# Two buffers for the mix's tile, 25-row stores as 24 and 1, and weights converted in 8 chunks

## The chip, the cores and the metric

The kernel runs on one core of one Trainium2 chip. The metric is the device time of one execution in microseconds (us). Five engines work side by side, each in the order of its own instruction list: TensorE (PE, with its weight loads as PEld), VectorE (DVE), ScalarE (ACT), GpSimd (POOL) and SyncE (SP), which here issues every DMA. An instruction that waits holds up all that stand behind it on its engine.

## The reference, cut to what matters

```python
X = rfft(x, axis=1)                        # x: 8 x 3136 x 256
Yr = shrink(Xr @ w_r - Xi @ w_i + b_r)     # shrink: towards zero by 0.01
Yi = shrink(Xr @ w_i + Xi @ w_r + b_i)
y  = irfft(Yr + 1j*Yi, n=3136, axis=1)
mixed = real(fft(fft(y, axis=1), axis=2))
u  = y + mixed
un = (u - mean(u)) / sqrt(var(u) + 1e-6)   # over the 256 features
out = u + relu(un @ w_ch1) @ w_ch2         # 256 -> 1024 -> 256, weights float64
```

The sequence transform of y is Y itself, so `mixed` needs only a transform of Y over the 256 features. The two MLP weights come as float64 and are turned on the chip into a high and a low float32r part.

## The kernel before, in words

The length 3136 is factored as 64 x 49. Each of 8 batches (b) goes through ten generators, one per stage:

- `p1`: the 64-point transform. A chunk of `x` is loaded into `xf`, multiplied (`g_f`), copied to `ev` and stored to a DRAM array `ad` (L348 to L367). For batch 0 it is `p1_first` (L279 to L334), whose copies use borrowed tiles, the tags `uth`, `utl` and `W0` among them. From each copy the first eight frequencies are stored at once and the rest later (the `rest` stores, L333).
- `p2_f2`: the 49-point transform, in four quarters q of eight frequencies. `af` and `tff` are loaded (L400, L402), the product `g_f` (L416) is split into `Xh`, `Xl`, `Xsh`, `Xsl`. The tiles come from `x_tiles`: in quarters 1 and 3 of batch 0 they are borrowed, the two `Xh` from tag `uth` (written by L429), the two `Xl` from `utl`.
- `p2_w`: the complex weights, bias and shrink, giving `Y` (L470 to L481).
- `p2_mix`: the feature transform of Y, for `mixed`. Even and odd parts (`ef` or `eo`, L516), four products `g_mix` (L535 to L540), each copied into a quarter of the tile `mq` (by ACT at L542 in batch 0, by DVE at L546 after), sums and differences (L548 to L557), and stores of `mq` into the DRAM array `md` (L562 to L574).
- `p2_yt`, `p2_g2`: transposes of Y and the inverse 49-point transform, `bev`, stored to `bd` (L637).
- `p3_norm`: loads `bf` from `bd` (L664) and `mt` from `md` (L668, L670), the inverse 64-point transform `g_g`, the sum `ut` (L678), the normalization (L683 to L695).
- `p3_tr`, `p3_mlp1`, `p3_mlp2`: transposes into `uth`, `utl` (tags of the same names, two buffers each, L705), the two MLP products (`h` and `o`), the sum and the output store (L752, L754).

`weights` (L756) drives `split_double` (L158) for the float64 weights: 16 chunks of 256 columns each. A chunk is loaded as pairs of 32-bit words into `raw` (tag `bf`, two buffers, L166), eight DVE instructions work on the words (L169 to L182), ACT makes the high part (L183), POOL the low part (L185, L186). `behind(1, ...)` puts the load on SP behind the load of batch 0's second `af` tile.

Order. Every generator yields due times in units of T (a batch takes 1.0 T in steady state, and the weights lie at 1.2 T to 1.7 T); a heap emits the instructions in the order of the due times (L774 to L780). The tile framework then plans each engine's list from that sequence with a simulated timeline, takes a buffer of a tag when one is free, and puts in the semaphores. So the order of each engine's list is a result of planned times, and tags with a fixed number of buffers are what a tile waits for. Stores and loads share SP's one queue.

The lines of `x_tiles` that borrow:

```python
if b == 0 and q % 2:
    return [[sb.tile([128, 8] + c + [S], F32R, tag=t + z, bufs=2, ...) for k in range(2)]
            for t, c in (("ut", [2]), ("b", [])) for z in "hl"]
```

Of the kernel before, what the change touches and what calls it, by code (L numbers as in the profile page):

```python
# [10 lines left out]
F32 = mybir.dt.float32  # L11
F32R = mybir.dt.float32r
I32 = mybir.dt.int32
AF = mybir.ActivationFunctionType
ALU = mybir.AluOpType
# [104 lines left out]
T = 10000  # L120
# [8 lines left out]
def spectral_block(ctx: ExitStack, tc: tile.TileContext, x, w_ri, b_ri, w1, w2,  # L129
# [3 lines left out]
    va, sc, gp, te = nc.vector, nc.scalar, nc.gpsimd, nc.tensor  # L133
# [21 lines left out]
    st_eng = nc.sync  # L155


    def split_double(name, h, l, sl, src):  # L158

        def tmp(tag, bufs, dt=I32):
            return sb.tile([128, 256], dt, tag=tag, bufs=bufs, name=f"cv_{name}_{tag}")

        raw = sb.tile([128, 512], I32, tag="bf", bufs=2, name="raw_" + name)
        behind(1, out=raw, in_=src)  # L166
        lo, hi = raw[:, 0::2], raw[:, 1::2]
        t = tmp("mt", 2)
        va.tensor_scalar(t, hi, 0x7FFFFFFF, None, op0=ALU.bitwise_and)  # L169
        tf = t.bitcast(F32)  # L170
        va.tensor_scalar(tf, tf, HI_MIN, HI_MAX, op0=ALU.max, op1=ALU.min)
        va.tensor_scalar(t, t, 3, 0x7FFFFFFF, op0=ALU.logical_shift_left, op1=ALU.bitwise_and)
        w = tmp("ut", UTB)
        va.tensor_scalar(w, hi, -0x80000000, 0x40000000, op0=ALU.bitwise_and, op1=ALU.bitwise_or)
        va.tensor_tensor(w, w, t, op=ALU.bitwise_xor)
        wf = w.bitcast(F32)
        e = tmp("ut", UTB)
        va.tensor_scalar(e, w, -0x800000, None, op0=ALU.bitwise_and)
        r = tmp("mt", 2)
        va.tensor_scalar(r, lo, 8, None, op0=ALU.logical_shift_right)  # L180
        rf = tmp("ut", UTB, F32)
        va.scalar_tensor_tensor(rf, r, 2.0 ** -44, e.bitcast(F32), op0=ALU.mult, op1=ALU.mult)  # L182
        sc.copy(h[sl], wf)  # L183
        d = tmp("ut", UTB, F32)
        gp.tensor_sub(d, wf, h[sl].bitcast(F32))  # L185
        gp.tensor_add(l[sl], d, rf)  # L186


    fwd_f = cp.tile([128, 128], F32, name="fwd_f")
# [65 lines left out]
    def behind(key, **kw):  # L255

        assert key in af_ld
        with tc.issue_after(af_ld[key]):
            return nc.sync.dma_start(**kw)
# [227 lines left out]
    def p2_mix(b):  # L487


        md = dr.tile([2 * (NH + 64), D], F32, tag="md", bufs=4, name=f"md{b}")  # L490
        mpd, mmd = m_dram[b] = md[0:NH + 64], md[NH + 64:]
        both = md[0:2 * (NH + 63)].rearrange("(a r) d -> a r d", a=2)

        def rows(d, first, nj, n):

            return d[first:first + 64 * nj].rearrange("(j k) d -> j k d", k=64)[:, 0:n]

        def rows2(first, nj):
            return both[:, first:first + 64 * nj].rearrange("a (j k) d -> j a (k d)", k=64)[:, :, 0:4 * D]
        for q in range(4):  # L500
            base, STEP, F2W, W0, WW, M0 = clock2(b, q)
            u0 = 8 * q
            yield base + STEP * M0
            y = yt_[b, q]
            if b == 0:
                ef = sb.tile([128, 2, 8, S], F32, tag=("eh", "el")[q % 2], bufs=1, name="ef")
            else:
                eh = sb.tile([128, 2, 4, 100], F32R, tag="eh", bufs=1, name="eh")
                el = sb.tile([128, 2, 4, 100], F32R, tag="el", bufs=1, name="el")


            sets = ((np.s_[:], np.s_[:25]), (np.s_[::-1], np.s_[25:]))
            for e in range(2):
                eo = sb.tile([128, 8, S], F32, tag="eo", bufs=2, name="eo") if b else ef[:, e]
                for ru, js in sets:
                    va.scalar_tensor_tensor(eo[:, :, js], y[:, 1, ru, e, js], mask[:, e:e + 1],  # L516
                                            y[:, 0, ru, e, js], op0=ALU.mult, op1=ALU.add)
                    if e:
                        sc.copy(eo[0:1, :, js], y[0:1, 1, ru, 0, js])
                if b:  # L520
                    eov = eo.rearrange("p (u s) j -> p u (s j)", s=2)
                    sc.copy(eh[:, e], eov)
                    lo_v(el[:, e], eov, eh[:, e])

            mq = sb.tile([100, 2, 4, 2, 128], F32, tag="mq", bufs=1, name="mq")
            even, odd = mq[:, 1, :, 0], mq[:, 1, :, 1]
            for ui in range(4):
                yield base + STEP * (M0 + 0.372 + 0.394 * ui / 2)
                g = gtile("g_mix")
                gv = g[:100].rearrange("p (c h e) -> p c h e", c=2, h=2)  # L530
                for e in range(2):
                    o = g[:100, e * 256:e * 256 + 256]
                    n = (129, 128)[e]
                    if b == 0:
                        te.matmul(o[:, :n], ef[:, e, 2 * ui:2 * ui + 2].rearrange("p s j -> p (s j)"), KF["cs"][:, e, :n], start=True, stop=True)  # L535
                    else:
                        cs = K["cs"][:, e].rearrange("p h e -> p (h e)")
                        te.matmul(o, eh[:, e, ui], cs, start=e == 0, stop=False)
                        n += n % 2
                        te.matmul(o[:, :n], el[:, e, ui], cs[:, :n], start=False, stop=e == 1)  # L540
                if b == 0:
                    sc.copy(mq[:, 1, ui], gv[:, :, 0])  # L542
                else:
                    low = lows[ui % 2]
                    sc.copy(low[:, :, 1:], gv[:, :, 1, 1:])
                    va.tensor_add(mq[:, 1, ui], gv[:, :, 0], low)  # L546

                va.tensor_add(mq[:, 0, ui, 1, 0:1], gv[:, 0, 1, 0:1], odd[:, ui, 0:1])  # L548

            for i, f in ((0, va.tensor_add), (1, va.tensor_sub)):  # L550
                f(even[:, :, i::2], even[:, :, i::2], odd[:, :, 0:1].to_broadcast((100, 4, 64)))
            gp.tensor_add(mq[:, 0, :, 0, 1:], even[:, :, 1:], odd[:, :, 1:])
            gp.tensor_sub(mq[:, 0, :, 1, 1:], even[:, :, 1:], odd[:, :, 1:])
            sc.copy(mq[:, 0, :, 0, 0:1], even[:, :, 0:1])
            sc.copy(even[:, :, 1:], mq[:, 0, :, 1, 1:])
            va.tensor_copy(odd[:, :, 1:], mq[:, 0, :, 0, 1:])
            sc.copy(odd[:, :, 0:1], mq[:, 0, :, 1, 0:1])  # L557
            mr = mq.rearrange("p a u h e -> p a (u h e)")
            mp, mm = (mq[:, i].rearrange("p u h e -> p u (h e)") for i in range(2))

            if q:
                st_eng.dma_start(out=rows2(u0, 25), in_=mr[0:25])  # L562
                st_eng.dma_start(out=rows2(61 - u0, 24), in_=mr[75:99])
            else:
                st_eng.dma_start(out=rows(mpd, 0, 25, 4), in_=mp[0:25])
                st_eng.dma_start(out=rows(mmd, 0, 25, 3), in_=mm[0:25, 1:4])
                st_eng.dma_start(out=rows(mpd, 61, 24, 3), in_=mp[75:99, 0:3])
                st_eng.dma_start(out=rows(mmd, 60, 24, 3), in_=mm[75:99, 0:3])

                st_eng.dma_start(out=rows(mmd, 63, 24, 1), in_=mm[1:25, 0:1])  # L570
                st_eng.dma_start(out=rows(mpd, 32, 24, 1), in_=mp[75:99, 3:4])
                st_eng.dma_start(out=rows(mmd, 31, 25, 1), in_=mm[75:100, 3:4])
            st_eng.dma_start(out=rows2(u0 + 4, 25), in_=mr[50:75])
            st_eng.dma_start(out=rows2(57 - u0, 24), in_=mr[25:49])  # L574
        done.add(("m", b))

# [177 lines left out]
                st_eng.dma_start(out=out[b // 2, :, slot:slot + n, :], in_=ut[:, :n])  # L754

    def weights():  # L756
        w1v = w1.bitcast(I32).rearrange("(k p) f -> k p f", p=128)
        w2v = w2.bitcast(I32).rearrange("(f p) e -> f p e", p=128)
        parts1 = [(np.s_[:, k, q * 256:q * 256 + 256], w1v[k, :, q * 512:q * 512 + 512])
                  for k in range(2) for q in range(4)]  # L760
        parts2 = [(np.s_[:, f, :], w2v[f]) for f in range(8)]
        for i, (name, shape, loads) in enumerate((("w1", [128, 2, FF], parts1), ("w2", [128, 8, D], parts2))):
            h = sb.tile(shape, F32R, tag=f"W{2 * i}", bufs=1, name=name + "h")
            l = sb.tile(shape, F32R, tag=f"W{2 * i + 1}", bufs=1, name=name + "l")
            mlp_w[name] = h, l
            for j, (sl, src) in enumerate(loads):
                yield T * (1.2 + 0.5 * (8 * i + j) / 16)
                split_double(name, h, l, sl, src)


# [47 lines left out]
```

## Time and profile before

| | |
|---|---|
| median of 3 runs | 1977.26 us (1976.86 to 1981.97) |
| profiled execution | 1975.88 us, span 1974.1 us |
| PE busy | 1861.2 us (94%) |
| DVE / ACT / POOL busy | 1330.2 (67%) / 850.3 (43%) / 710.1 us (36%) |
| chain that ended last | PE 80%, DMA 7%, DVE 7%, SP 2% |

The busy line of PE in 40 slices of 49.4 us each, in tenths, shows the two phases of the kernel:

```profile
PE   4875799989999999999999999999999999999999
```

The first five slices (some 250 us) hold the load of batch 0, the conversion of the weights and the first passes of batches 0 and 1. From then on PE is busy nearly all the time. Time is the end of the last instruction, so an idle microsecond of PE counts where no other idle stretch swallows it, and an idle microsecond of another engine counts only where PE waits in the end.

### The profile page before, as it was taken

What the parts mean: (1) busy time and instruction counts of PE and PEld (TensorE: products, weight loads), DVE (VectorE), ACT (ScalarE), POOL (GpSimd) and SP (SyncE); (2) the same over time, 40 slices, a digit from 0 to 9 for tenths busy, and PEclk for the clock granted to TensorE, in tenths of its full rate; (3) what the DMA queues carried; (4) which work ended last, traced back from release to release, by engine and by line L of the source; (5) the groups of instructions that cost most, each with busy time, mean ns of one, the idle gap of its engine ahead of it and who ended that gap; (6) DMA issues with size and microseconds to landing.
All of it is one profiled execution on the core that took longest, in us unless ns stands there. A gap on an engine that the chain in (4) does not pass through costs nothing.

```text
span 1974.1 us, 35182 instructions
## 1 busy us (share of the span) xinstructions
PE 1861.2 (94%) x12115; PEld 1709.3 (87%) x12115; DVE 1330.2 (67%) x2903; ACT 850.3 (43%) x1888; POOL 710.1 (36%) x1103
## 2 busy tenths in 40 slices
PE   4875799989999999999999999999999999999999
PEld 2754699979999899998999899998999989998999
DVE  3973777767766776766667776766677766675543
ACT  2443454435444544444444444444544434433322
POOL 1534544344333444333333443323433322322110
PEclk7896899999999999999999999999999999999999
DMA  8466544344343543435443454435433333223210
GB/s 222 127 173 186 155 135 128 95 113 141 111 137 97 148 135 109 117 108 141 135 135 102 121 144 111 128 101 144 135 105 98 106 96 89 83 70 107 68 41 25
DMA packets 163677, 233.06 MB, mean 118 GB/s; under 512 B 27108, under 2 KB 107052, under 8 KB 163500
## 3 DMA queue, kind: packets, MB, share of 16 engines
q1 hardware_dynamic: 163500, 230.81, 41.4%
q8 instruction: 97, 1.59, 0.3%
q14 instruction: 80, 0.66, 0.1%
HBM read 127.95 MB, written 102.76 MB: 117 GB/s over the span
## 4 chain that ended last, share of the span: by engine, by line
PE 80%; DMA 7%; DVE 7%; SPq 2%; issue 1%; ACT 1%; POOL 0%; DVEq 0%; ACTq 0%; POOLq 0%
PE o L151 9%; PE o L150 9%; PE o L152 8%; PE h L150 8%; PE h L152 8%; PE h L151 8%; PE g_f L416 4%; PE g_w L150 3%; PE g_w L151 3%; PE g_w L152 3%; PE g_g L150 2%; PE g_g L152 2%; PE g_g L151 2%; PE g_yt L604 2%; PE g_ut L713 2%; DMA md<-mq 2%
## 5 line engine op out<-in xcount | busy, mean ns | idle before, releaser
L733 DVE SCALAR_TENSOR_TENSOR hl<-h,hh 128x512 fp32r<-128x512 f32 (+1 forms) x416 | 272.4, 655 | 255.7 <-ACT hh L732 254.6
L151 PE MATMUL o<-w2h,hl 128*128 128x256 f32 x1568 | 433.5, 285 | 9.7 <-DVE hl L733 9.6
L732 ACT ACTIVATE hh<-h 128x512 fp32r<-128x512 f32 (+1 forms) x416 | 237.7, 572 | 450.6 <-PE h L152 387.6
L152 PE MATMUL o<-w2h,hh 128*128 128x256 f32 x1568 | 426.1, 281 | 0.0
L150 PE MATMUL o<-w2l,hh 128*128 128x256 f32 x1568 | 398.4, 287 | 8.1 <-ACT hh L732 5.3
L150 PE MATMUL h<-utl,w1h 128*128 128x512 f32 (+1 forms) x832 | 324.6, 390 | 6.4 <-DVE hl L733 6.4
L152 PE MATMUL h<-uth,w1h 128*128 128x512 f32 (+1 forms) x832 | 318.1, 382 | 0.0
L151 PE MATMUL h<-uth,w1l 128*128 128x512 f32 (+1 forms) x832 | 316.9, 381 | 0.0
L151 PEld LDWEIGHTS o<-w2h,hl 128*128 128x128 f32 x1568 | 296.3, 189 | 16.6 <-DVE hl L733 12.1
L150 PEld LDWEIGHTS o<-w2l,hh 128*128 128x128 f32 x1568 | 286.0, 189 | 21.7 <-ACT hh L732 6.6
L152 PEld LDWEIGHTS o<-w2h,hh 128*128 128x128 f32 x1568 | 296.1, 189 | 3.3
L147 POOL TENSOR_TENSOR bl<-bf,bh 128x512 fp32r<-128x512 f32 x104 | 130.1, 1252 | 292.7 <-ACT bh L673 292.6
L416 PE MATMUL g_f<-tff,af 98*128 98x100 f32 x1024 | 152.6, 280 | 32.3 <-DMA af<-ad 16.6
L416 PEld LDWEIGHTS g_f<-tff,af 98*128 98x128 f32 x1024 | 145.0, 200 | 41.9 <-issue 29.0
L152 PEld LDWEIGHTS h<-uth,w1h 128*128 128x128 f32 x832 | 157.0, 189 | 24.9
L147 POOL TENSOR_TENSOR xl<-xf,xh 128x512 fp32r<-128x512 f32 (+1 forms) x75 | 97.4, 1298 | 221.6 <-ACT xh L359 213.4
L150 PEld LDWEIGHTS h<-utl,w1h 128*128 128x128 f32 x832 | 157.2, 189 | 20.9 <-DVE hl L733 7.2
L151 PEld LDWEIGHTS h<-uth,w1l 128*128 128x128 f32 x832 | 157.3, 189 | 13.6
L678 DVE TENSOR_TENSOR ut<-g_g,mt 128x512 f32<-128x512 f32 x104 | 68.3, 657 | 106.8 <-PE g_g L152 68.1
L147 POOL TENSOR_TENSOR Xsl<-xs,Xsh 128x200 fp32r<-128x200 f32 x120 | 77.4, 645 | 155.3 <-ACT Xsh L425 132.6
L147 POOL TENSOR_TENSOR Xl<-xx,Xh 128x400 fp32r<-128x400 f32 (+1 forms) x96 | 106.8, 1115 | 71.5 <-ACT Xh L425 67.8
L695 DVE TENSOR_SCALAR mt<-ut,ag,rs 128x256 f32<-128x256 f32 x196 | 90.8, 502 | 46.2 <-POOL rs L693 45.9
(155 smaller groups left out, 3815.8 us busy)
## 6 DMA issues: line engine op xcount, KB each, us to landing
bd<-bev SPq DMA_DIRECT2D x128, 196.0 KB
af<-ad SPq DMA_DIRECT2D x62, 392.0 KB
bf<-bd SPq DMA_DIRECT2D x184, 128.0 KB
out_dram<-ut SPq DMA_DIRECT2D x92, 256.0 KB
xf<-in_x SPq DMA_DIRECT2D x176, 128.0 KB
ad<-ev SPq DMA_DIRECT2D x168, 128.0 KB
mt<-md SPq DMA_DIRECT2D x416, 32.0 KB
mt<-md SPq DMA_DIRECT2D x184, 64.0 KB
```

The costliest lines, as they stand in the source:

```text
L147: gp.tensor_sub(out_, full, hi.bitcast(F32))
L150: te.matmul(o, lh, rl, start=start, stop=False)
L151: te.matmul(o, ll, rh, start=False, stop=False)
L152: return te.matmul(o, lh, rh, start=False, stop=stop)
L416: te.matmul(g[:, o:o + 100], afs[s][:, ui * D + k * 128:ui * D + k * 128 + 128], tfs[s][:, ui], start=True, stop=True)
L604: te.transpose(gt[:100, (v * 2 + o) * 128:(v * 2 + o + 1) * 128], y[:, o, place].rearrange("p c j -> p (c j)"), ident)
L678: va.tensor_add(ut[:, :n], g[:, :w].rearrange("p (n d) -> p n d", d=D), mt[:, :n])
L695: va.tensor_scalar(mt[:, j], ut[:, j], ag[:, j, 0:1], rs[:, j], op0=ALU.subtract, op1=ALU.mult)
L713: te.transpose(gv[:, k, j * 128:(j + 1) * 128], mt[:, j, k * 128:(k + 1) * 128], ident)
L732: sc.activation(hh[:, :w], h[:, :w], AF.Relu)
L733: va.scalar_tensor_tensor(hl[:, :w], h[:, :w], 0.0, hh[:, :w].bitcast(F32), op0=ALU.max, op1=ALU.subtract)
```

## The change

Three edits. (1) The tile `mq` of the mix gets two buffers in place of one. (2) Each store of 25 rows of `mq` through `rows2` becomes a store of 24 rows and one of the last row: two of them in quarters 1 to 3, one in quarter 0. (3) The float64 weights are converted in 8 chunks of 512 columns in place of 16 of 256; the raw words lie in tag `uth` (4 KB a partition, two buffers) in place of `bf`; the absolute value is an ACT activation (Abs) in place of a DVE instruction, the other seven DVE instructions stay, with operands twice as long.

```diff
         def tmp(tag, bufs, dt=I32):
-            return sb.tile([128, 256], dt, tag=tag, bufs=bufs, ...)
-        raw = sb.tile([128, 512], I32, tag="bf", bufs=2, name="raw_" + name)
-        behind(1, out=raw, in_=src)
+            return sb.tile([128, 512], dt, tag=tag, bufs=bufs, ...)
+        raw = sb.tile([128, 1024], I32, tag="uth", bufs=2, name="raw_" + name)
+        behind(1, out=raw.rearrange("p (f e) -> p f e", f=src.shape[1]), in_=src)
         lo, hi = raw[:, 0::2], raw[:, 1::2]
-        t = tmp("mt", 2)
-        va.tensor_scalar(t, hi, 0x7FFFFFFF, None, op0=ALU.bitwise_and)
-        tf = t.bitcast(F32)
+        tf = tmp("mt", 2, F32)
+        sc.activation(tf, hi.bitcast(F32), AF.Abs)
         va.tensor_scalar(tf, tf, HI_MIN, HI_MAX, op0=ALU.max, op1=ALU.min)
+        t = tf.bitcast(I32)
...
-            mq = sb.tile([100, 2, 4, 2, 128], F32, tag="mq", bufs=1, name="mq")
+            mq = sb.tile([100, 2, 4, 2, 128], F32, tag="mq", bufs=2, name="mq")
...
             if q:
-                st_eng.dma_start(out=rows2(u0, 25), in_=mr[0:25])
+                st_eng.dma_start(out=rows2(u0, 24), in_=mr[0:24])
+                st_eng.dma_start(out=rows2(u0 + 64 * 24, 1), in_=mr[24:25])
                 st_eng.dma_start(out=rows2(61 - u0, 24), in_=mr[75:99])
...
-            st_eng.dma_start(out=rows2(u0 + 4, 25), in_=mr[50:75])
+            st_eng.dma_start(out=rows2(u0 + 4, 24), in_=mr[50:74])
+            st_eng.dma_start(out=rows2(u0 + 4 + 64 * 24, 1), in_=mr[74:75])
...
-        parts1 = [(np.s_[:, k, q * 256:q * 256 + 256], w1v[k, :, q * 512:q * 512 + 512])
-                  for k in range(2) for q in range(4)]
-        parts2 = [(np.s_[:, f, :], w2v[f]) for f in range(8)]
+        parts1 = [(np.s_[:, k, q * 512:q * 512 + 512], w1v[:, k:k + 1, q * 1024:q * 1024 + 1024])
+                  for k in range(2) for q in range(2)]
+        parts2 = [(np.s_[:, f:f + 2, :], w2v[:, f:f + 2]) for f in range(0, 8, 2)]
...
-                yield T * (1.2 + 0.5 * (8 * i + j) / 16)
+                yield T * (1.2 + 0.5 * (4 * i + j) / 8)
```

## Rows read from the trace of the kernel before

**Rows 1.** Stretches: PE, PEld, DVE, ACT, POOL busy us (instructions), clock, DMA share, GB/s.

```profile
38.00:50.00 12.00, 0.08 (x1) 0.00 (x0) 7.02 (x20) 2.60 (x9) 5.72 (x9) 0.50 0.86 234
50.00:117.00 67.00, 53.37 (x288) 46.12 (x288) 62.44 (x151) 33.94 (x96) 38.73 (x53) 0.91 0.47 131
117.00:157.00 40.00, 29.24 (x125) 20.76 (x126) 28.97 (x75) 16.15 (x40) 14.15 (x14) 0.84 0.65 184
157.00:210.00 53.00, 25.55 (x94) 19.77 (x94) 13.26 (x24) 17.66 (x37) 17.89 (x22) 0.63 0.67 183
250.00:1974.00 1724.00, 1694.55 (x11314) 1575.60 (x11312) 1177.99 (x2551) 748.06 (x1640) 611.57 (x969) 0.99 0.39 110
```

**Rows 2.** The tile mq: waits before its instructions (us, times); one in time.

```profile
  DMA md<-mq: 7.4, 3
...
137.95 0.37 ACT L542 COPY mq<-g_mix 100x256 f32<-100x256 f32 x1 [3.72 <-DMA md<-mq]
```

**Rows 3.** Chain of waits, first and last conversion piece: start us, us, what.

```profile
53.83 0.29 DVE cv_w_mt L169
...
106.48 0.49 DVE cv_w_mt L171
```

**Rows 4.** DVE in order of time: start us, us, line, operation, shapes.

```profile
43.78 0.29 DVE L171 TENSOR_SCALAR cv_w_mt<-cv_w_mt 128x256 f32<-128x256 f32 x1
...
44.43 0.43 DVE L175 TENSOR_TENSOR cv_w_ut<-cv_w_ut,cv_w_mt 128x256 int32<-128x256 int32 x1
...
79.59 0.56 DVE L481 TENSOR_TENSOR Y<-y,m 128x400 f32<-128x400 f32 x1
...
80.82 0.35 DVE L480 TENSOR_SCALAR m<-y 128x400 f32<-128x400 f32 x1
```

**Rows 5.** ACT groups, 0 to 260 us: busy us, mean ns, idle before.

```profile
L359 ACT CAST xh<-xf 128x512 fp32r<-128x512 f32 x9 | 5.6, 619 | 10.4 <-PE g_f L152 5.6 <-DMA xf<-in_x 4.8
...
L183 ACT CAST w1h<-cv_w_ut 128x256 fp32r<-128x256 f32 x8 | 3.3, 410 | 10.6 <-DVE cv_w_ut L175 10.6
...
L686 ACT ACT_TABLE_LOAD x1 | 1.3, 1283 | 0.0
```

**Rows 6.** Chain of waits: the store to md that ended last, and what follows.

```profile
190.66 5.59 DMA md<-mq
...
198.48 1.84 DMA mt<-md
...
883.62 5.82 DMA md<-mq
...
1781.69 5.60 DMA md<-mq
```

**Rows 7.** SP's issues of stores from mq: one, and all of L574 (ns, min/median/max).

```profile
131.57 0.40 SPq L573 DMA_DIRECT2D md<-mq  x1
...
L574 SPq DMA_DIRECT2D md<-mq x32: 328/1466/1832, 109.3 to 1781.7; - x32
```

**Rows 8.** Chain of waits: other transfers of 196 KB and 256 KB.

```profile
43.89 9.91 DMA raw_w<-in_w
...
167.50 1.92 DMA bd<-bev
```

**Rows 9.** PE in order of time, with its idle time before.

```profile
50.29 1.15 PE L416 MATMUL g_f<-tff,af 98*128 98x100 f32 x4 [12.21 <-DMA af<-ad]
...
89.69 0.35 PE L152 MATMUL g_w<-Xh,wdh 128*128 128x400 f32 x1
...
208.25 0.66 PE L713 MATMUL g_ut<-ident,mt 128*128 128x128 f32 x2 [11.80 <-DMA xf<-in_x]
```

**Rows 10.** ACT's first writes of quarters 1 and 3, in order of time.

```profile
57.23 1.14 ACT L429 CAST Xh<-xx 128x200 fp32r<-128x200 f32 x4
...
94.27 0.63 ACT L429 CAST Xh<-xx 128x200 fp32r<-128x200 f32 x2
```

**Rows 11.** SP in order of time around the first raw loads.

```profile
38.87 0.85 SPq L259 DMA_DIRECT2D raw_w<-in_w  x2
```

More of the change, by code (lines that the diff above doesn't have):

```diff
@@ L162, in tmp @@
         def tmp(tag, bufs, dt=I32):
-            return sb.tile([128, 256], dt, tag=tag, bufs=bufs, name=f"cv_{name}_{tag}")
-        raw = sb.tile([128, 512], I32, tag="bf", bufs=2, name="raw_" + name)
-        behind(1, out=raw, in_=src)
+            return sb.tile([128, 512], dt, tag=tag, bufs=bufs, name=f"cv_{name}_{tag}")
+        raw = sb.tile([128, 1024], I32, tag="uth", bufs=2, name="raw_" + name)
+        behind(1, out=raw.rearrange("p (f e) -> p f e", f=src.shape[1]), in_=src)
         lo, hi = raw[:, 0::2], raw[:, 1::2]
-        t = tmp("mt", 2)
-        va.tensor_scalar(t, hi, 0x7FFFFFFF, None, op0=ALU.bitwise_and)
-        tf = t.bitcast(F32)
+        tf = tmp("mt", 2, F32)
+        sc.activation(tf, hi.bitcast(F32), AF.Abs)
         va.tensor_scalar(tf, tf, HI_MIN, HI_MAX, op0=ALU.max, op1=ALU.min)
+        t = tf.bitcast(I32)
         va.tensor_scalar(t, t, 3, 0x7FFFFFFF, op0=ALU.logical_shift_left, op1=ALU.bitwise_and)
@@ L182, in split_double, with v @@
         va.scalar_tensor_tensor(rf, r, 2.0 ** -44, e.bitcast(F32), op0=ALU.mult, op1=ALU.mult)
-        sc.copy(h[sl], wf)
+        def v(t):
+            return t.rearrange("p (f e) -> p f e", f=h[sl].shape[1]) if len(h[sl].shape) == 3 else t
+        sc.copy(h[sl], v(wf))
         d = tmp("ut", UTB, F32)
-        gp.tensor_sub(d, wf, h[sl].bitcast(F32))
-        gp.tensor_add(l[sl], d, rf)
+        gp.tensor_sub(v(d), v(wf), h[sl].bitcast(F32))
+        gp.tensor_add(l[sl], v(d), v(rf))
     fwd_f = cp.tile([128, 128], F32, name="fwd_f")
@@ L756, in weights @@
     def weights():
-        w1v = w1.bitcast(I32).rearrange("(k p) f -> k p f", p=128)
-        w2v = w2.bitcast(I32).rearrange("(f p) e -> f p e", p=128)
-        parts1 = [(np.s_[:, k, q * 256:q * 256 + 256], w1v[k, :, q * 512:q * 512 + 512])
-                  for k in range(2) for q in range(4)]
-        parts2 = [(np.s_[:, f, :], w2v[f]) for f in range(8)]
+        w1v = w1.bitcast(I32).rearrange("(k p) f -> p k f", p=128)
+        w2v = w2.bitcast(I32).rearrange("(f p) e -> p f e", p=128)
+        parts1 = [(np.s_[:, k, q * 512:q * 512 + 512], w1v[:, k:k + 1, q * 1024:q * 1024 + 1024])
+                  for k in range(2) for q in range(2)]
+        parts2 = [(np.s_[:, f:f + 2, :], w2v[:, f:f + 2]) for f in range(0, 8, 2)]
         for i, (name, shape, loads) in enumerate((("w1", [128, 2, FF], parts1), ("w2", [128, 8, D], parts2))):
```

## The prediction

> **What bounds the kernel now.** I first cut the span into stretches to see where TensorE is idle [rows 1]. After 250 us it is busy 1694.6 of 1724 us, so only 29.4 us can be won there. Before that it idles 11.9 us in 38 to 50, 13.6 in 50 to 117, 10.8 in 117 to 157 and 27.4 in 157 to 210. The change works mostly in these 172 us, which hold all conversions and the four mixes of batch 0, so I went on with the chain of waits and the engines' instructions in order of time there.
>
> Each stretch has its own limit. From 38 to 50 PE stands before L416 until `af` lands, 12.2 us [rows 9], while the DMA engines are 86% busy at 234 GB/s [rows 1]. From 50 to 117 DVE is busy 62.4 of 67 us [rows 1], and the chain runs through it, conversion instructions among them [rows 3]. From 117 to 210 DVE is mostly idle and the chain hops from one latency to the next: transfers, ACT copies, PSUM buffers. Three times there ACT stands at L542, 7.4 us in all, for the stores of the quarter before to leave the one `mq` tile [rows 2]. Behind L542 on ACT stand copies that free PSUM for PE. The stretch ends with PE idle for 11.8 us until 208.3 [rows 9]. The row names an `xf` load, but what L713 reads is the normalized `mt`, and the chain goes through the last store to `md` (5.6 us), the `mt` loads and the normalization to that instruction [rows 6].
>
> **The change part by part.** The sum is made against the profiled execution, 1975.9 us (span 1974.1 and 1.8 around it), 1.4 us below the median of 1977.3.
>
> *Two `mq` buffers.* The three waits at L542 can only be 0 or as long as now, since the second buffer was last stored two quarters before. Of the 7.4 us nothing to everything reaches the end; what is late next is PE itself, whose `g_mix` products come right before each wait. I take all 7.4, because in these stretches no engine is full [rows 1]. After batch 0 no wait for this tile appears in its list [rows 2], so nothing is won there.
>
> *Stores of 24 and 1.* The last store of a quarter takes 5.6 to 5.8 us from issue to landing [rows 6]. It carries 192 KB, and 196 KB from `bev` landed in 1.92 us [rows 8], so what it waits for is the 25-row stores ahead, as does its issue: L574 takes 1.47 us at the median where L573 took 0.40 [rows 7]. The gain per quarter lies between 0 (the stores ahead are as slow as before) and 3.7 us (5.6 less 1.9). I take 2.5, nearer to the `bev` row, less 0.8 for two more issues at 0.40 ahead of the last one: 1.7. It counts once in the start, where the `mt` loads wait for it, since the two buffers cover the other three quarters. In steady state three such stores lie on the chain, the first at 883.6 and the last at 1781.7 [rows 6]; most of their time is beside PE work, and I take 1.5 for them together, out of bounds of 0 and 3 x 3.7 = 11. The 56 more issues (7 in each of 8 batches) cost SP 56 x 0.40 = 22 us over the span; they are hidden as long as the loads behind them are early, which PE's 98% after 250 us says.
>
> [...]
>
> *Conversions on DVE.* A tensor-scalar instruction takes 0.29 us on 256 columns and 0.35 on 400, a two-tensor one 0.43 and 0.56 [rows 4]. Straight on, 512 columns take 0.40 and 0.66. Two old chunks cost 2 x (6 x 0.29 + 2 x 0.43) = 5.2 us, a new one 5 x 0.40 + 2 x 0.66 = 3.3, 0.63 of it, so DVE is relieved of 8 x 1.9 = 15 us. On the chain lie 19 pieces of conversions, 10.6 us together [rows 3]; 0.37 of that is 3.9. Bounds are 0 and 15; I take 3.5, since others of DVE's instructions that are now ahead can be held by POOL or ACT instead.
>
> *Abs on ACT.* It adds 8 x 0.62 us [L359, rows 5], and copies of 512 columns in place of 256 save 16 x 0.41 - 8 x 0.62 = 1.6: 3.4 us more on an engine that is busy half the time from 50 to 117 [rows 1]. New is that L171 waits for ACT, with all of DVE's list behind it. ACT no longer stands at L542, so I cost this at 0; if the cover is gone it is some 0.6 us a chunk, 5 in all. A function that ACT's tables lack would cost 1.28 us [rows 5] per change, up to 16 times, 20 us. Relu, copies and casts run without one, and I take 0. [...]
>
> *Loads of 512 KB.* The first two raw loads are issued at 38.87 [rows 11], ahead of the `af` loads for which PE stands until 50.3 [rows 9]. They carry 512 KB more in total, at 234 GB/s [rows 1] 2.2 us later for PE: +2.2, between 0 (the `af` loads are planned first) and 2.2.
>
> *Raw words in `uth`.* Quarter 1 of batch 0 takes both `uth` buffers from 57.2 [rows 10] until PE's last read at 89.7 [rows 9], quarter 3 from 94.3 on [rows 10]. Loads and quarters now take turns. A quarter that comes late waits on ACT, at L429, with everything on ACT behind it. The bounds are 0 and, by the second rival, 25.6; I take +2, as before 57 and between 89.7 and 94.3 there is time for one pair each.
>
> Sum: -7.4 - 1.7 - 1.5 - 3.5 + 2.2 + 2 = -9.9, hence 1966 us.
>
> **The rivals.** [...]
>
> (b) *Slower: the turns at `uth`.* The planner takes a free buffer for the next raw pair before quarter 1 writes. Chunks 2 and 3 are then issued at some 48 us, when chunks 0 and 1 are converted, land after 9.9 us, as the third load did [rows 8], plus 2.2 for the doubled size, and take 2 x 3.3 = 6.6 us to convert if DVE does nothing else, 13.2 if other work has half of it: they end at 66.7 to 73.3, against L429's 57.2 [rows 10], 9.5 to 16.1 us lost on ACT, 12.8 in the middle. The same in front of quarter 3 makes 25.6. The gains without these turns are 14.1, less 2.2 for `af` 11.9: where the two delays exceed 11.9 together the kernel is slower. At 25.6 it takes 1975.9 + 13.7 = 1989.6. Against it: DVE is the limit there anyway, so that part of the delay is beside its work.
>
> (c) *No change.* The waits at L542 go, but the `g_f`, `ad`, `af` round trip of batch 1 was as late, and PE's 27.4 idle us stay; the conversions' relief is eaten by the later `af`. Then -3.5 - 1.7 + 2.2 + 2 = -1, 1975. For it speaks that PE stands for `af` and not for `mq` at the ends of these stretches [rows 9].
>
> Since each engine's list is planned anew, some shift of either sign comes with each case; I allow 5 us.
>
> **How the numbers follow.** My forecast has 0.45, (a) 0.20, (c) 0.20, (b) 0.15. A measurement tells about 0.3% (5.9 us) from no change, that is below 1971.4 or above 1983.2 against the median. The forecast with its 5 us is faster in 0.42 and the same in 0.03; (a) is faster; (c) is the same in 0.17 and slower in 0.03; (b) is slower in 0.13 and the same in 0.02. This makes faster 0.62, same 0.22, slower 0.16. The range goes from (a) less the 5 us, 1949, to 1982, which takes in (c) with more than 5 us and leaves out most of (b).
>
> **What would show it.** Right: no wait of L542 for `md<-mq`; the last store of a quarter landing in 3 to 4 us; 7 DVE instructions a chunk near 0.40 and 0.66 us; PE's first `h` product some 8 to 11 us earlier than before, the rest of the span as long as now. Wrong: ACT standing at L429 for a conversion, `raw_w` in SP's waits ahead of `af`, a table load beside Abs, or PE's idle time after 250 us changed by more than 5 us, which would mean that the new plan and not the edits decides.

## The result and the profile after the change

The changed kernel takes 1960.01 us (median of 4 runs, 1956.38 to 1963.65) against 1977.06 us of the kernel before (4 runs, 1975.35 to 1981.97): a ratio of 0.991, with an interval of 0.9883 to 0.9936, or 17 us. The forecast was 1966 us, 11 below the median. The profiled execution took 1961.45 us with a span of 1959.7, 14.4 us less than the span before. One execution among all runs below, of 2452 us where the others of its kernel took 580 to 584, is left out as disturbed. The time did not come from where the sum had it, so the views are read again in the same order.

The stretches of the changed kernel, to be held against [rows 1], with the same columns:

```profile
50.00:117.00 67.00, 54.90 (x286) 48.64 (x286) 48.92 (x100) 34.38 (x95) 28.08 (x38) 0.86 0.48 138
...
157.00:210.00 53.00, 25.52 (x90) 19.54 (x90) 25.11 (x40) 19.64 (x43) 25.47 (x26) 0.60 0.64 176
250.00:1959.00 1709.00, 1684.81 (x11316) 1569.11 (x11314) 1177.96 (x2551) 748.85 (x1641) 611.54 (x969) 1.00 0.40 111
```

DVE is relieved from 50 to 117, 48.9 us in place of 62.4, but PE is no busier for it from 157 to 210, 25.5 us in both. After 250 us the same work (11316 PE instructions, 11314 before) takes 1709 us instead of 1724, and PE's idle time there falls from 29.4 to 24.2 us, the other 9.7 of the 15 being a shorter busy time. In this execution the start gives nothing and all of the gain lies in steady state.

The chain of waits, with the rows that answer to [rows 6] and what stands ahead of the first of them:

```profile
82.12 5.88 DMA raw_w<-in_w
...
185.99 5.82 DVE mq L559
191.87 0.32 SPq L565
...
194.42 3.82 DMA md<-mq
...
208.63 0.66 PE g_ut L718 x2
...
418.58 3.31 DMA md<-mq
```

The last store of a quarter now lands in 3.3 to 3.95 us where it took 5.6 to 5.8. In the start this is worth nothing here, because the store is issued 3.8 us later: 2.3 us of that come from the DVE copy of L559 (L556 before), which took 5.82 us, and 1.4 from the two more issues. The copy in the chain before:

```profile
187.72 1.75 DVE mq L556
```

L718 (L713 before) starts at 208.63, against 208.25 [rows 9].

What ACT waited for at L545 (L542 before) from 60 to 215 us, to be held against [rows 2]; the row for `md<-mq` is gone from the view:

```profile
ACT mq L545 <- PE g_mix L538: 5.9, 4, 5.1
...
ACT Xh L432 <- DVE cv_w_mt L180: 2.5, 2, 2.3
```

The issues of the one-row store of L578 and of the last store, against [rows 7] (ns, min/median/max):

```profile
L578 SPq DMA_DIRECT2D md<-mq x32: 592/615/663, 101.4 to 1769.6; - x32
L579 SPq DMA_DIRECT2D md<-mq x32: 411/644/810, 102.1 to 1770.2; - x32
```

The last issue fell from 1.47 us to 0.64 at the median, and a one-row store costs 0.62 instead of the 0.40 of the forecast.

SP and PE in the start, against [rows 9] and [rows 11]:

```profile
39.99 1.28 SPq L403 DMA_DIRECT2D af<-ad  x3
...
46.43 1.15 PE L419 MATMUL g_f<-tff,af 98*128 98x100 f32 x4 [8.55 <-DMA af<-ad]
```

The raw words did not go ahead of `af`. Their first load is issued at 82.12 us (in the chain above), after quarter 1 has used `uth`, so `af` is 3.9 us earlier for PE, not 2.2 later, and the conversions' loads start 43 us later than before.

The costliest group of conversion instructions, 30 to 260 us (busy us, mean ns), of the kernel before:

```profile
L182 DVE SCALAR_TENSOR_TENSOR cv_w_ut<-cv_w_mt,cv_w_ut 128x256 f32<-128x256 int32 x16 | 9.8, 612 | 0.2
```

and of the changed one, with the Abs:

```profile
L182 DVE SCALAR_TENSOR_TENSOR cv_w_ut<-cv_w_mt,cv_w_ut 128x512 f32<-128x512 int32 x8 | 7.8, 970 | 0.1
...
L169 ACT ACTIVATE cv_w_mt<-raw_w 128x512 f32<-128x512 f32 x8 | 5.4, 678 | 3.6 <-DMA raw_w<-in_w 3.0 <-DVE cv_w_ut L182 0.6
```

All eight DVE groups of this view sum to 54.4 us before and the seven after to 42.2: 12.2 us of relief where 15 were worked out from undisturbed rows. Abs takes 0.68 us and no further table load appears.

### The profile page after: what moved, and what is told of

The parts are those of the page before. It is cut to its first block, busy times and chain, and to the rows that moved or that the text cites. A ratio compares the mean times of both kernels' runs of the same rounds, so it can differ in the third digit from the quotient of the medians.

```text
span 1959.7 us, 35047 instructions
## 1 busy us (share of the span) xinstructions
PE 1856.2 (95%) x12115; PEld 1709.1 (87%) x12115; DVE 1322.5 (67%) x2831; ACT 853.2 (44%) x1888; POOL 704.8 (36%) x1087
## 4 chain that ended last, share of the span: by engine, by line
PE 80%; DVE 7%; DMA 6%; SPq 3%; issue 2%; ACT 1%; POOL 1%; DVEq 0%; POOLq 0%; ACTq 0%
PE o L150 8%; PE o L151 8%; PE o L152 8%; PE h L150 8%; PE h L151 8%; PE h L152 8%; PE g_f L419 4%; PE g_w L150 3%; PE g_w L152 3%; PE g_w L151 3%; PE g_g L150 2%; PE g_g L152 2%; PE g_g L151 2%; PE g_yt L609 2%; PE g_ut L718 2%
## 5 line engine op out<-in xcount | busy, mean ns | idle before, releaser
L700 DVE TENSOR_SCALAR mt<-ut,ag,rs 128x256 f32<-128x256 f32 x196 | 90.8, 502 | 48.9 <-POOL rs L698 48.6
```

The lines of the kernel that those rows point to most:

```text
L700: va.tensor_scalar(mt[:, j], ut[:, j], ag[:, j, 0:1], rs[:, j], op0=ALU.subtract, op1=ALU.mult)
```

## The experiments

Three things were to be told apart: what each edit is worth alone, whether the forecast's largest term (the buffers) is real, and whether the new plan of instructions rather than the edits decides, which was the last of the prediction's wrong signs.

**The stores alone.**

```diff
-                st_eng.dma_start(out=rows2(u0, 25), in_=mr[0:25])
+                st_eng.dma_start(out=rows2(u0, 24), in_=mr[0:24])
+                st_eng.dma_start(out=rows2(u0 + 64 * 24, 1), in_=mr[24:25])
```

and the same for the store of `mr[50:75]`.

> Edit 2 alone: the 25-row stores as 24 and 1, one mq buffer, 16 weight chunks as before. The whole change took 17 us off (ratio 0.991). Theory A (the prediction's steps): the start carries the gain, the stores are worth 1.7 + 1.5 = 3 us, ratio 0.998. Theory B (from the two traces: both reach the first output store at 271 us and the gain comes after, from 405 us on, where loads of mt wait for stores to md): the stores carry it, 10 to 17 us, ratio 0.991 to 0.995. Theory C (any edit makes a new plan, and the plan decides): no relation to either; a gain or loss of some 5 to 10 us for each edit that does not add up.

Measured: 1968.3 us (1965.25 to 1970.55) against 1977.29, a ratio of 0.995 (0.9938 to 0.9961), 9.0 us. Nearly three times the 3.2 us of the forecast, from one edit.

**The two buffers alone.**

```diff
-            mq = sb.tile([100, 2, 4, 2, 128], F32, tag="mq", bufs=1, name="mq")
+            mq = sb.tile([100, 2, 4, 2, 128], F32, tag="mq", bufs=2, name="mq")
```

> Edit 1 alone: two mq buffers, stores and weights as before. Theory A: the waits at the copy into mq go, 7.4 us, ratio 0.996. Theory B: the waits go, but the start ends no earlier; within 3 us of before, ratio 0.9985 to 1.0015. Theory C: anything within 10 us.

Measured: 1980.11 us (1977.49 to 1982.78), a ratio of 1.0014 (1.0005 to 1.0023), 2.8 us slower. The lists of instructions are the same as before on every engine after 260 us. The trace shows where the 7.4 us went. What ACT waited for from 60 to 215 us, in this kernel:

```profile
ACT bev L635 <- PE g_g L631: 14.1, 8, 5.2
ACT Xsh L425 <- DVE xs L438: 10.2, 4, 5.2
ACT mq L542 <- PE g_mix L535: 8.3, 5, 4.2
...
ACT ev L363 <- PE g_f L355: 4.8, 3, 4.1
```

The same four waits of the kernel before:

```profile
ACT bev L635 <- PE g_g L631: 11.9, 7, 5.6
ACT Xsh L425 <- DVE xs L438: 8.2, 3, 5.1
...
ACT mq L542 <- PE g_mix L535: 5.3, 4, 3.4
...
ACT ev L363 <- PE g_f L355: 2.0, 3, 1.4
```

The 7.4 us for the stores are gone, and 10.0 have come back in these four, the largest that grew. All of ACT's waits in this stretch sum to 87.8 us before and 90.0 here. The chain at the end of the start:

```profile
192.04 5.52 DMA md<-mq
...
209.87 0.66 PE g_ut L713 x2
```

The stretch ends 1.6 us later than before.

**The conversions alone.** The change without the edits to `mq` and its stores:

```diff
-        va.tensor_scalar(t, hi, 0x7FFFFFFF, None, op0=ALU.bitwise_and)
+        sc.activation(tf, hi.bitcast(F32), AF.Abs)
...
-        raw = sb.tile([128, 512], I32, tag="bf", bufs=2, name="raw_" + name)
+        raw = sb.tile([128, 1024], I32, tag="uth", bufs=2, name="raw_" + name)
```

> Edit 3 alone: weights in 8 chunks with Abs on ACT and raw words in uth, one mq buffer, 25-row stores as before. Theory A: -3.5 + 2.2 + 2 = +0.7 us, ratio 1.000. Theory B: the same 1.000 within 3 us, as PE ends the start at the same time whatever DVE saves. Theory C: anything within 10 us.

Measured: 1970.36 us (1964.4 to 1975.84, 7 runs), a ratio of 0.9956 (0.9939 to 0.9972), 6.9 us. The lists differ from before in the start only.

**The price of a store by its rows.** The stores of `mq` alone, each waited for, and the groups of a quarter:

```diff
+    for n in (25, 24, 23, 20, 16, 12, 1):
+        case(f"one{n}", [(8, 0, n)])
+    case("four_old", [(8, 0, 25), (53, 75, 24), (12, 50, 25), (49, 25, 24)])
+    case("four_new", [(8, 0, 24), (8 + 64 * 24, 24, 1), (53, 75, 24), (12, 50, 24), (12 + 64 * 24, 74, 1), (49, 25, 24)])
```

> A kernel that does none of the computation: from one tile it stores 25, 24, 23, 20, 16, 12 and 1 rows of 2 x 4 KB to DRAM with the strides of the mix's stores, each alone and four times over, then the old four stores of a quarter (25, 24, 25, 24), the new six (24, 1, 24, 24, 1, 24) and four of 24; after each group a VectorE write of the tile waits until all have landed. [...] If time goes by bytes alone, 25, 24 and 23 rows differ by under 10% and the six take longer than the four by their two issues, 0.8 us.

Measured, in the chain of waits (start us, us from issue to landing; 25, 24, 23, 20 and 1 rows in this order, then the last store of the old and of the new group):

```profile
76.80 2.94 DMA one<-mq
...
86.23 2.44 DMA one<-mq
...
96.89 8.53 DMA one<-mq
...
131.95 2.42 DMA one<-mq
...
164.15 1.95 DMA one<-mq
...
173.57 5.38 DMA four_old<-mq
...
208.65 3.04 DMA four_new<-mq
```

By itself a store of 25 rows costs only 0.5 us more than one of 24; it is in a group that it costs. From the first issue to the last landing the old four stores take 6.5 to 7.0 us in four repetitions and the new six 5.5 to 5.8, two more issues included. Landing is not in order of size: 23 rows take 8.53 us, and 16 and 12 rows 2.50 and 2.45. Why 23 rows take so long is not shown; the DMA engines that carry a store have no names in the trace.

**More of the same cost.** The kernel before, its 25 rows as 23 and 2:

```diff
-                st_eng.dma_start(out=rows2(u0, 25), in_=mr[0:25])
+                st_eng.dma_start(out=rows2(u0, 23), in_=mr[0:23])
+                st_eng.dma_start(out=rows2(u0 + 64 * 23, 2), in_=mr[23:25])
```

and the same for `mr[50:75]`.

> The kernel before with each 25-row store as 23 and 2 rows in place of 25: the same bytes and the same number of issues as 24 and 1. Alone, a 23-row store landed after 8.5 us where 24 rows took 2.4 and 25 took 2.9. If the landing of the stores to md carries the gain (theory B), this kernel is slower than before by some 3 to 6 us at each of the boundaries where mt loads wait, 10 to 30 us in all, ratio 1.005 to 1.015. If the new plan or the mere splitting does it, it is as fast as 24 and 1, ratio 0.995.

Measured: 2149.41 us (2144.08 to 2151.82) against 1976.35, a ratio of 1.0869 (1.0849 to 1.0888): 173 us slower. The direction was as expected and the size far off. Its chain of waits and DVE's waits:

```profile
369.57 14.12 DMA md<-mq
```

```profile
DVE mq L546 <- DMA md<-mq: 75.1, 13, 9.8
```

The last store lands in 14.1 us here, in 13 to 16 at 17 of its 19 places on the chain, and with one buffer DVE now stands for it 75 us in 13 places, a wait that has no row after batch 0 before the change. On the chain `md<-mq` has 11.8% of 2146.9 us, 253 us, where it had 38 of 1974.1. So this time is a price on the path, and a store's row count alone moves the kernel by 9% when it is chosen badly.

**Two edits at a time, and all three again.** The change with one `mq` buffer, the change with the old stores, and the change itself, on one chip:

> Edits 2 and 3 without edit 1: stores as 24 and 1, weights in 8 chunks, one mq buffer. Alone, edit 2 gave a ratio of 0.995, edit 3 0.9956 and edit 1 1.0014. If the edits add up, this is 0.9906 against before and 0.9986 against the whole change, some 1957 to 1959 us, the fastest version. If the plan decides (theory C), it can be anywhere within 10 us of the whole change.

> Edits 1 and 3 without edit 2: 25-row stores as before. Adding up: 0.9956 x 1.0014 = 0.997, some 1971 us, so that undoing the stores alone gives back 10 us of the 17. Theory C: no sum holds.

> The whole change again, on the same chip as the others, for the interval: 0.989 to 0.993 by the first timing; 0.992 if the three edits' ratios multiply.

Measured against 1976.35: without the second buffer 1962.55 us (1954.78 to 1963.92), 0.992 (0.9902 to 0.9938); with the old stores 1968.76 us (1958.09 to 1971.74), 0.9952 (0.9934 to 0.9971); the whole 1959.13 us (1956.16 to 1963.39), 0.9909 (0.9893 to 0.9926). The second buffer is worth 3.4 us in this company with intervals that overlap by most of their width, the stores 9.6 us. The three ratios alone multiply to 0.995 x 1.0014 x 0.9956 = 0.992. So the forecast's largest term, the buffers, is not there, and a plan that decides apart from the edits is not needed for the sum of the medians.

Where the difference arises is seen in the start of the output stores, in us against the kernel before (one profiled execution each):

```
output store            6th   11th   16th   21st   31st   41st   61st   last
stores alone            1.7   -4.3   -4.3   -9.8   -5.7   -5.5   -5.9  -10.6
no second buffer        1.3   -2.9   -3.3   -9.2   -5.5   -6.5   -8.1  -13.4
whole change            0.4   -7.5   -7.9  -13.7  -10.3   -8.1  -11.2  -14.8
whole change again     -3.5   -9.2   -9.6  -15.6  -11.5   -8.0  -10.9  -17.1
two buffers alone       1.5    1.6    1.6    1.5    1.5    3.4    3.8    5.8
conversions alone       4.9    0.7    0.3   -0.1   -0.7    0.8   -1.6   -5.1
with the old stores    -5.2   -9.3   -9.6   -9.7  -10.3   -9.2  -11.4  -17.8
```

The executions of one kernel differ by up to 14 us, and the profiled one with the old stores is the fastest of its seven, 10.7 us below their median: a row is one course of its kernel, not its mean.

From the 16th to the 21st store every kernel with the new stores gains 5.5 to 6.0 us and every one without them at most 0.4. This is a batch boundary, where the `mt` loads of one batch wait for the mix's last store. Most of it is a store that leaves earlier and not work that ends earlier: by the 31st 1.4 to 2.4 us are left, and PE itself, held against the kernel before instruction by instruction, is 0.9 to 1.6 us earlier behind this boundary than ahead of it (700 against 655 us), in the kernels without the new stores 0.2 at most.

From the 6th to the 11th lies another boundary. There, the stretches (columns as in [rows 1]) of the kernel before:

```profile
405.00:440.00 35.00, 29.63 (x174) 25.58 (x174) 23.42 (x42) 14.68 (x34) 18.20 (x23) 0.92 0.46 128
...
434.00:440.00 6.00, 5.38 (x18) 4.60 (x19) 2.68 (x6) 1.21 (x3) 2.29 (x6) 0.51 0.81 226
```

of the stores alone:

```profile
405.00:440.00 35.00, 32.26 (x215) 28.83 (x214) 24.91 (x47) 17.11 (x39) 19.71 (x26) 1.00 0.47 130
...
433.00:440.00 7.00, 6.32 (x46) 5.89 (x47) 3.00 (x8) 2.33 (x5) 2.53 (x6) 1.00 0.69 205
```

PE's instruction at the end of its gap, in order of time, of the kernel before:

```profile
434.52 0.80 PE L150 MATMUL o<-w2l,hh 128*128 128x256 f32 x2 [3.51 <-ACT hh L732]
```

of the stores alone:

```profile
433.68 0.39 PE L151 MATMUL o<-w2h,hl 128*128 128x256 f32 x1 [1.54 <-DVE hl L735]
```

Before, and with the two buffers alone, PE stands 3.5 and 3.8 us, and behind that gap its clock is granted at 0.50 to 0.51: 18 instructions take 5.4 us. With the stores alone it stands 1.5 us and the clock stays at 1.00: 46 instructions take 6.3. From 405 to 440 PE gets through 215 instructions instead of 174. At the 333 in 50 us that it does undisturbed (450 to 500 us of the kernel before) the 41 more are 6.2 us, and the table has 6.0.

The new stores are not what decides on the clock, though. Without the second buffer they are in, and the clock falls to 0.50 behind a shorter gap:

```profile
433.55 0.39 PE L151 MATMUL o<-w2h,hl 128*128 128x256 f32 x1 [1.87 <-DVE hl L738]
...
435.00:438.00 3.00, 3.00 (x10) 2.47 (x9) 0.51 (x2) 0.58 (x2) 0.00 (x0) 0.50 0.62 185
```

With the old stores and the conversions it stays at 1.00 here, from 405 to 440 us, and at a later boundary behind a gap of 3.31 us:

```profile
1346.39 0.50 PE L150 MATMUL h<-utl,w1h 128*128 128x512 f32 x1 [3.31 <-DVE hl L736]
...
1344.00:1352.00 8.00, 5.61 (x43) 5.34 (x44) 6.40 (x16) 3.50 (x8) 2.19 (x6) 1.00 0.71 198
```

From 250 us on, the last 20 us left out, PE is at a granted clock of 0.50 for 17.1 us before, 6.8 with the stores alone, 13.6 with the conversions alone and in both executions of the whole change, and 3.4 with the old stores. So at the first boundary the shorter gap goes with the new stores (1.9 us at most, 2.4 at the least without them), and whether the clock falls behind it differs from kernel to kernel.

The conversions gain in another way. The same 1364 PE instructions, in a stretch in which neither PE's idle time nor its clock differs, of the kernel before:

```profile
450.00:655.00 205.00, 203.48 (x1364) 189.67 (x1362) 152.22 (x326) 95.36 (x214) 83.29 (x129) 1.00 0.43 120
```

of the stores alone, and of the conversions alone:

```profile
445.70:650.70 205.00, 203.49 (x1364) 189.72 (x1362) 152.17 (x326) 95.50 (x214) 83.48 (x129) 1.00 0.44 122
...
450.70:655.00 204.30, 202.71 (x1364) 189.06 (x1362) 151.94 (x326) 95.40 (x214) 83.23 (x129) 1.00 0.43 120
```

Nearly all of the 0.77 us lies in the 516 products `o` of the second MLP step, 73.58 us in place of 74.27. In five such stretches with 910 us together (450 to 655, 700 to 880, 930 to 1100, 1150 to 1340 and 1400 to 1565 of the kernel before) PE gains 3.4 to 3.6 us in each of the five profiles with the conversions (the whole change twice), and 0.0 with the stores or the two buffers alone. By length that is an estimate of some 6 us over the whole steady state, which is about what the conversions measured alone. Why the same instructions run closer together is open; the edit gives the shared tiles other sizes, and where tiles lie in memory is not in the traces.

**A kernel of two batches.** The kernel before, with the conversions alone, and the whole change:

> The kernel before with 2 of its 8 batches (batches 2 to 7 are left out), so that the start weighs more and most of the steady state is gone; the reference point for the next two. By the full kernel's trace the second batch's output ends some 500 us into it; without the work of later batches beside it, 400 to 480 us.

> Edit 3 alone, with 2 of 8 batches. In the full kernel edit 3 alone was 7 us faster, and its lists of instructions differ from those of before in the start alone. If its gain arises in the start (DVE relieved, or the loads of the weights moved behind those of af), this kernel is 5 to 8 us faster than the 2-batch kernel before. If the gain arises later, by how the same lists fall against each other and against the clock, it is within 2 us of it.

> The whole change with 2 of 8 batches. If the stores gain at every boundary between batches (8.5 us over 8 batches), here only one or two of these are left: 1 to 3 us below the 2-batch kernel with edit 3 alone. By the prediction's steps, which put 13 of 14 us into the start, it would be 10 us or more below the 2-batch kernel before.

Measured: 583.29 us (581.79 to 587.67), 581.3 (580.49 to 584.15) and 574.97 (570.22 to 577.06). The conversions give 2.0 us here, within the spread of the executions and not the 5 to 8 that were expected if their gain lay in the start. So the larger part of their 6.9 us arises later, in batches whose instructions the edit leaves as they were, as the stretches above show. The whole change gives 8.3, 6.3 of it beyond the conversions, where 1 to 3 were expected: in one profile of each PE is already 5.1 us earlier at 300 us, so more of it lies in the start than in the full kernel's profiles, and by which edit was not taken apart.

**The copy in front of the stores.** In the changed kernel the start hangs on L559. POOL and the copy in that place, in order of time:

```profile
185.91 1.02 POOL L147 TENSOR_TENSOR Xl<-xx,Xh 128x400 fp32r<-128x400 f32 x1
...
189.02 2.50 POOL L147 TENSOR_TENSOR bl<-bf,bh 128x512 fp32r<-128x512 f32 x2
...
185.99 5.81 DVE L559 COPY mq<-mq 100x508 f32<-100x508 f32 x1 [1.16 <-POOL mq L556]
```

The copy has a median of 0.42 us. Here it lasts as long as POOL's instructions follow each other without a gap, to 191.5. It is not the only place: in the second execution of the change it took 5.81 us at 182.0, and at the first boundary 4.05 us in the kernel before, at 414.3. Moved to ACT:

```diff
-            va.tensor_copy(odd[:, :, 1:], mq[:, 0, :, 0, 1:])
+            sc.copy(odd[:, :, 1:], mq[:, 0, :, 0, 1:])
```

> The whole change, and the last copy of the mix (odd from the sums, L559) moved from DVE to ACT. In the trace of the whole change this DVE copy took 0.41 us at the median and up to 5.81, ending when POOL's run of instructions ended; it stands right before the stores to md, for which the mt loads wait at the end of the start and at the boundaries. On ACT such a copy takes 0.62 us (L558). If the hold by POOL is what makes the stores late, the start ends up to 5 us earlier and the boundaries gain too: 5 to 12 us below the whole change, some 1950 us. If ACT's own list makes it as late, within 3 us of the whole change, 1957 to 1962.

Measured: 1947.74 us (1941.61 to 1949.13) against 1974.54, a ratio of 0.9861 (0.9843 to 0.988). That beats both kernels: 27 us below the one before and, by the ratios, 0.0048 or some 9 us below the changed one. Its chain:

```profile
181.94 0.53 ACT mq L559
182.53 0.32 SPq L565
...
185.33 3.53 DMA md<-mq
...
199.41 0.66 PE g_ut L718 x2
```

The stores leave 9.3 us earlier than in the changed kernel (182.53 for 191.87) and L718 starts 9.2 us earlier, 5.0 earlier than in that kernel's second execution (204.39). The move also gave PE another order of instructions after 260 us, so that all 9 us come from the copy is not shown.

## Why the prediction was right or wrong, point by point

**Direction and size.** The time is faster and inside the range, at 17 us for 11. Against the terms, this is errors that partly cancel, so that the total came out near is in part luck. Rival (a), which the low end of the range (1949 us) was taken from, did not come. It rested on a higher granted clock from 157 to 210 us, a term that no run of the change shows: in its profile the clock is 0.60 there in place of 0.63, with PE busy for 25.5 us in both.

**The two buffers, -7.4.** This step failed. The waits vanished as forecast, but nothing of them reached the end: +2.8 us alone, -3.4 in company, the latter not clear of the noise. The step had named what is late next, `g_mix` of PE right before each wait, and then took the whole 7.4 "because in these stretches no engine is full". That no engine is full says only that latencies decide there. It does not say that ACT has other work ready once this wait is gone: ACT stood for PE and DVE instead, 10.0 us more in four waits in place of 7.4, and its waits as a whole did not shrink. The chain did run through the stores, but a chain names the one release that came last and not the one a few hundred ns behind it. This is the premise of rival (c), and it was right on this term.

**The stores, -3.2 together.** The mechanism was right: 3.3 to 3.95 us to landing, inside the forecast 3 to 4. The term was mis-sized, with 9.0 us alone and 9.6 in company. The start was priced at 1.7 and steady state at 1.5, out of bounds of 0 and 11 there. The step priced what the chain showed of the stores, and read "most of their time is beside PE work" from PE's 98%. It missed that a late store ended in a gap of PE (3.51 us at the first boundary), and that the granted clock fell to 0.51 behind it: with the stores alone, 2 us less of a gap and a clock that did not fall gave 6 us at the first boundary. How often the clock falls is not set by the stores alone, so this share of the 9 us is read from single executions. The 3.1 us to landing (5.6 less 2.5) that the step took from the `bev` row was short of the measured 3.3 to 3.95.

**The conversions, -3.5, and `uth`, +2 and +2.2.** Forecast +0.7 together, measured -6.9 alone, so this block was wrong in sign. DVE was relieved by 12.2 us, 0.8 of what was worked out: the five tensor-scalar instructions took 0.42 to 0.95 us mean and the two others 0.75 and 0.97, not 0.40 and 0.66. One of them, L174, took 0.41 at the least and 1.50 at the most, so 0.40 is the undisturbed time; what held the others was not tried. The chain of the kernel before has 35 pieces of conversions with 13.3 us from 53.8 us on, where the prediction counted 19 with 10.6; its 0.37 is 4.9 and not 3.9. None of the relief reached the end of the start: in the profile of the conversions alone L718 starts at 211.24, 3.0 us later than before. `af` came 3.9 us earlier in the whole change, because quarter 1 took `uth` first and the loads fell behind `af`; the turns thus went the other way round from rival (b), and ACT stood at L432 for conversions for 2.5 us in all, at most 2.3 at a time. The price is the raw load on the chain at 82 us (5.88), and the conversions after it. The step that failed is the one that looked for this edit's gain in DVE's list and on the chain of the start. What the runs show in its place is PE running the same products closer together through all of the steady state, some 6 us by the estimate above, a term that the sum did not have. In the one profile of the conversions alone the clock also stays at 1.00 behind the first boundary's gap of 2.41 us, where the table has 4.2 us of gain, and falls at a later boundary where it did not fall before (0.95 from 870 to 905 us in place of 1.00).

**The sign that was listed as wrong.** PE's idle time after 250 us did change by more than 5 us (29.4 to 24.2). It did not mean what the prediction had it mean: the two-at-a-time kernels add up as the single ones do, within their intervals. Another such sign came, ACT standing at L432 for conversions. Of the signs of being right, DVE's instructions did not come near 0.40 and 0.66 us, and PE's first `h` product, forecast 8 to 11 us earlier, starts at 223.85 us against 223.34 before (220.04 in the second execution), while the rest of the span, forecast as long as before, is shorter by the whole gain.

**The sum.** -9.0 + 2.8 - 6.9 is -13.1, the whole is -17.0 and -17.2 in its two comparisons. The missing 4 us lie within the intervals of the three (about 3 us to each side), and so remain unexplained.

## What to carry to other kernels

Before pricing a wait that an edit removes, ask which wait would end last then; here the removed one stood beside another round trip and gave nothing. Price a store that others wait for by the landing of its whole group, measured with the row counts in use, and look at the boundaries between batches, where here a late landing became a gap of PE (3.51 us at the first one) and at times a stretch at a granted clock of 0.50. Hold the same instructions of both kernels against each other where nothing waits: a gain there belongs to no wait. Then look at what stands right ahead of such a store: moving a copy of 0.4 us there gave as much as the best of the three edits.

## What the runs showed of the hardware that was not expected

A store of 23 rows lands in 8.53 us where 24 rows take 2.44 and 20 take 2.42; in the kernel this made 173 us.

A DVE copy of 100 x 508 elements took 0.41 us at the least and 5.81 at the most. The longest ran from 185.99 to 191.80 us, while POOL went through six instructions from 185.91 to 191.52; before the change the same copy got through in 1.82 us with POOL running on to 192.4. What held it and what let it in was not tried; on ACT it took 0.61 us at the median and 0.62 at the most.

At the first boundary the granted clock fell to 0.50 or 0.51 behind gaps of PE of 3.51, 3.83 and 1.87 us, each in another kernel, and stayed at 1.00 behind 1.54 and 2.41 us in two others; at a later boundary it stayed at 1.00 behind 3.31 us. The length of the gap alone does not tell.

The same 1364 PE instructions, with the same idle time and at a granted clock of 1.00, took 203.48 us in the kernel before and 202.71 with the conversions alone, an edit that left PE's list after 130 us as it was.
